# Planning a kernel's order with longer elementwise steps, longer hops, later landings and new priorities

## The chip, the cores and the metric

The kernel runs on one core of one Trainium2 chip. The metric is device microseconds (us) of one execution; the time of a kernel is the median of its runs, and lower is better.

## The reference

Causal attention with a cumulative bias, then two feed-forward layers, all in float32. Batch 4, 8 heads, 576 positions, head width 64, so 2304 tokens of width 512; the feed-forward width is 2048.

```python
scores = scale * np.matmul(q, k.transpose(0, 1, 3, 2))
cum = np.cumsum(np.maximum(s, 0.0), axis=-1)
bias = -(cum[:, :, :, None] - cum[:, :, None, :])
scores = np.where(causal, -1000000000.0, scores + np.minimum(bias, 0.0))
attn = softmax(scores); x = attn @ v           # heads side by side: 2304 x 512
h = x @ w_in;  x = (h * clip(h + 3, 0, 6) / 6) @ w_out       # layer 1
h = x @ w2_in; out = mish(h) @ w2_out                        # layer 2
```

## The kernel before

The tokens are laid out in an order of their own, in five blocks of 512, 512, 384, 512 and 384 tokens. Blocks 0 and 1 hold positions 0 to 255 of the four batches (two batches each), blocks 2 to 4 positions 256 to 575.

**Attention** goes by pairs of heads. `small` (L572) does a pair for positions 0 to 255: scores on TensorE (L610), bias and row minimum on VectorE (L622), exponentials on ScalarE (L629), a reciprocal (L637, L638), the division by it on either engine (L647 ScalarE, L649 VectorE), transposes on TensorE (L655), their copies out of PSUM (L290 or L294), the product with V (L664), and a copy of its result into the block as a high and a low half (L290, L674). GpSimd masks the bias (L596) that a DMA has brought from the scratch tensor `cums`. `unit` (L424) does the same for positions 256 to 575 (scores L486, minimum L493, exponentials L501, transposes L532, V product L555); its result goes out to the scratch tensor `xs` (L568) and comes back into a block (L697).

**Layers.** A weight slice of 128 x 512 comes as 64-bit words and is split into a high and a low part by `load_split` (L328): L339 or L341, L345, L349, L355, then L290 or L294, L365. A slice has 16 numbers f; the first layer's come through `load_win` (L377) and `load_wo1`. `moe_step` (L713) does one slice of one block: the first product, four chunks of three matmuls (L722), the nonlinearity on ScalarE and VectorE (L733, L735 and L740, then L290 or L294, L743), and the second product, again chunks of three (L755 in layer 1, L760 in layer 2). Chunk c of the first product needs rows c of the block, that is head pair c of both batches in it. The chunks of the first product are chained, so nothing of slice 1 starts before the last chunk of slice 0.

**The order.** Nothing is issued in the order of the source. `Plan` collects nodes, each with an engine or a choice of two, a cost in us, a priority (smaller is earlier) and buffers, and `run` (L116 on) simulates them greedily: whenever an engine is free in its simulation it takes the ready node of smallest priority. The order that comes out is the program's order on each engine; on the chip each engine then follows its order and waits on semaphores. The costs and the simulated clock go nowhere else. A node's end is start plus cost; a dependent node is ready after a table value for the pair of engines plus `HOP`; a DMA ends 0.907 us after its share of a simulated ring. In the first 60 simulated us matmuls cost 1.6 times as much. Elementwise costs come from formulas: `v1x(n)` is 0.069 + 0.00104 n, `act(n)` 0.094 + 0.000833 n; the table says 0.128 from VectorE to ScalarE and 0.2 from either to TensorE.

**Priorities** are counted in units of 128 token columns of one slice; a slice of a 512 block is 4 units. They come from the numbers T: head pair k of the first batch has -100 + 2 k `sm`, of the second -100 + 8 `sm` + 2 k `sm2`, weight slice f of w_in -100 + `w0` + `w1` f (its elementwise steps one less, its load four less). After these 8 pairs come six windows of pairs with start `p0` to `p5` and length `s0` to `s5`. In a pair, `upre`/`spre` place the loads and the preparation ahead of its scores, `uhalf`/`shalf` its transposes and `upost`/`spost` its V product behind them, in steps of that window; TensorE's nodes of attention count 5.322 (`pe`) less. First products of block 0 begin at priority -12, those of block 2 at 119.

The first three lines below set the priorities of the first 8 pairs and of the w_in slices (L827, L829), the rest those within a pair (L436, L437, L576).

```python
units(*u, PRO + 8 * k * T["sm"], T["sm2"] if k else T["sm"], n0, ...)
load_win(0, f, PRO + T["w0"] + T["w1"] * f, [n0])
pre = prio - T["upre"] * step
half, post = prio + T["uhalf"] * step, prio + T["upost"] * step
pre, half, post = prio - T["spre"] * step, prio + T["shalf"] * step, prio + T["spost"] * step
```

Of the kernel before, what the change touches and what calls it, by code (L numbers as in the profile page):

```python
# [31 lines left out]
CTOT = sum(CW)  # L32

T = dict(
    sm=3.895, sm2=5.532, w0=5.919, w1=9.308, cum=14.045, wo=0.564, blk0=27.645, blk1=12.97, wo2=44.236,
    wo2r=11.978, win2=5.088, g=30.578, upre=6.511, uhalf=1.145, upost=3.306, uv=0.304, spre=6.035, shalf=0.728,
    spost=1.158, pe=5.322, bias=2.302, la=3, la2=2, wp=11.079, p0=-8.796, p1=2.0, p2=2.856,
    p3=65.354, p4=87.114, p5=119.475, s0=30.881, s1=22.0, s2=23.277, s3=36.84, s4=66.006, s5=29.106,
)
HOP = 0.05  # L40
BIAS = {"DVE": T["bias"]}


# [23 lines left out]
class Plan:  # L67
# [56 lines left out]
    def run(self):  # L124
        for n in self.nodes:
            n.left = len(n.deps)
            n.ready = 0.0
            for d in n.deps:
                d.succ.append(n)
        self.turn = {}  # L130
        news = [(n.prio if b.key is None else b.key, n.seq, b) for n in self.nodes for b in n.new if not isinstance(b, Bank)]
        for _, _, b in sorted(news, key=lambda x: x[:2]):
            self.turn.setdefault(b.tag, collections.deque()).append(b)
        engines = sorted({e for n in self.nodes for e in n.eng})
        free = {e: 0.0 for e in engines}
        pool = []
        for n in self.nodes:
            if n.left == 0:
                pool.append(n)
        done = []  # L140
        now = 0.0
        order = []
        ring = 0.0
        left = len(self.nodes)
        pool.sort(key=lambda n: (n.prio, n.seq))
        while left:
            progress = True
            while progress:
                progress = False
                for n in pool:  # L150
                    if n.ready > now + 1e-9:
                        continue
                    best = None
                    for e, c in zip(n.eng, n.cost):
                        w = c * BIAS.get(e, 1.0)
                        w += 0.989 * max(0.0, free[e] - now)
                        if best is None or w < best[2]:
                            best = (e, c, w)
                    if best is None or free[best[0]] > now + 1e-9 or not self.can(n):
                        continue  # L160
                    self.take(n)
                    e, c, _ = best
                    if e == "PE" and now < 60.0:
                        c *= 1.6
                    free[e] = now + c
                    n.end = now + c
                    if e == "SP":
                        ring = max(now + 1.1, ring) + n.lat
                        n.end = ring + 0.907
                    else:  # L170
                        n.end += n.lat
                    n.on = e
                    order.append((n, e))
                    pool.remove(n)
                    heapq.heappush(done, (n.end, n.seq, 0, n))
                    heapq.heappush(done, (n.end + 0.252, n.seq, 1, n))
                    left -= 1
                    progress = True
                    break
            times = [t for t in free.values() if t > now + 1e-9]  # L180
            times += [n.ready for n in pool if n.ready > now + 1e-9]
            if done:
                times.append(max(done[0][0], now))
            if not times:
                raise RuntimeError("stuck: " + ", ".join(str((n.prio, n.eng, [b.tag for b in n.new])) for n in pool[:8]))
            now = min(times)
            changed = False
            while done and done[0][0] <= now + 1e-9:
                _, _, kind, n = heapq.heappop(done)
                if kind:  # L190
                    self.drop(n)
                    continue
                for m in n.succ:
                    m.left -= 1
                    m.ready = max(m.ready, n.end + (0.0 if n.on == "SP" else HOPS.get((n.on, m.eng[0]), 0.12) + HOP + m.slack))
                    if m.left == 0:
                        pool.append(m)
                        changed = True
            if changed:
                pool.sort(key=lambda n: (n.prio, n.seq))  # L200
        self.total = now
        self.order = order
        for n, e in order:
            for b in n.new:
                if isinstance(b, Bank):
                    b.t = self.bank_pool.tile([P, 512], F32, tag=f"b{b.tag}", name=f"b{b.tag}")
                else:
                    p = b.pool() if callable(b.pool) else b.pool
                    b.t = p.tile(b.shape, b.dtype, tag=b.tag, name=b.name)
            n.fn(e) if len(n.eng) > 1 else n.fn()  # L210
# [718 lines left out]
```

## Time and profile before

| | |
|---|---|
| median of 3 runs | 1002.32 us (1001.36 to 1003.06) |
| the profiled execution | 1003.14 us, span 1001.4 us |
| TensorE busy | 982.1 us of the span, 98% |
| VectorE, ScalarE busy | 462.4 us, 476.9 us (46%, 48%) |
| chain that ended last | TensorE 95%, VectorE 2%, DMA 1%, ScalarE 1% |

The span runs from the first to the last instruction of the profiled execution; the 1.7 us by which its time is longer lie around it. Engine names in rows: PE is TensorE's matmuls, PEld its weight loads, DVE VectorE, ACT ScalarE, POOL GpSimd, SP SyncE. An L number is a line of the kernel. A row says out<-in by the program's tile names; b is a PSUM bank.

### The profile page before, as it was taken

What the parts mean: (1) busy time and instruction counts of PE and PEld (TensorE: products, weight loads), DVE (VectorE), ACT (ScalarE), POOL (GpSimd) and SP (SyncE); (2) the same over time, 40 slices, a digit from 0 to 9 for tenths busy, and PEclk for the clock granted to TensorE, in tenths of its full rate; (3) what the DMA queues carried; (4) which work ended last, traced back from release to release, by engine and by line L of the source; (5) the groups of instructions that cost most, each with busy time, mean ns of one, the idle gap of its engine ahead of it and who ended that gap; (6) DMA issues with size and microseconds to landing.
All of it is one profiled execution on the core that took longest, in us unless ns stands there. A gap on an engine that the chain in (4) does not pass through costs nothing.

```text
span 1001.4 us, 13786 instructions
## 1 busy us (share of the span) xinstructions
PE 982.1 (98%) x5016; PEld 803.8 (80%) x5016; DVE 462.4 (46%) x1067; ACT 476.9 (48%) x1008; POOL 44.1 (4%) x102
## 2 busy tenths in 40 slices
PE   6899999999999999999999999999999999999998
PEld 3567777777777798888889998888888888888996
DVE  7898887754544455435228879612112112111111
ACT  5887778675665555644226556323123223122222
POOL 1111110100010101000000000000000000000000
PEclk9799999999999999999999999999999999999999
DMA  8676876887566777466237785202001101000101
GB/s 274 199 256 239 275 229 228 276 262 216 168 199 195 233 219 216 138 237 220 85 122 251 254 270 187 84 1 74 1 1 43 43 1 63 1 1 1 43 1 32
DMA packets 60355, 146.05 MB, mean 146 GB/s; under 512 B 8352, under 2 KB 22720, under 8 KB 60288
## 3 DMA queue, kind: packets, MB, share of 16 engines
q1 hardware_dynamic: 60288, 145.17, 44.6%
q8 instruction: 40, 0.66, 0.3%
q14 instruction: 27, 0.22, 0.1%
HBM read 121.84 MB, written 23.31 MB: 145 GB/s over the span
## 4 chain that ended last, share of the span: by engine, by line
PE 95%; DVE 2%; DMA 1%; ACT 1%; issue 0%; SPq 0%; DVEq 0%; ACTq 0%
PE b L722 40%; PE b L755 20%; PE b L760 20%; PE b L486 4%; PE b L555 4%; PE b L532 3%; PE b L610 2%; PE b L664 1%; PE b L655 1%; DMA xs<-st 1%; DMA blk<-xs 0%; PE b L613 0%; DVE g L622 0%; DMA pt<-in_s_dram 0%; DVE win L365 0%
## 5 line engine op out<-in xcount | busy, mean ns | idle before, releaser
L722 PE MATMUL b<-blk,win 128*128 128x512 f32 (+1 forms) x1920 | 505.5, 373 | 0.3 <-DMA blk<-xs 0.3
L722 PEld LDWEIGHTS b<-blk,win 128*128 128x128 f32 x1920 | 347.0, 188 | 58.6 <-issue 6.6
L755 PE MATMUL b<-g,wo 128*128 128x512 f32 (+1 forms) x960 | 258.7, 378 | 0.0
L755 PEld LDWEIGHTS b<-g,wo 128*128 128x128 f32 x960 | 170.3, 188 | 28.6 <-issue 8.4
L743 DVE TENSOR_TENSOR g<-e,g 128x512 fp32r<-128x512 f32 (+1 forms) x120 | 77.2, 644 | 214.4 <-ACT g L290 213.5
L740 ACT ACTIVATE e<-b 128x512 f32<-128x512 f32 (+1 forms) x80 | 44.4, 555 | 249.4 <-PE b L722 249.2
L760 PE MATMUL b<-wo,wo 128*128 128x512 f32 x432 | 122.1, 391 | 0.0
L760 PE MATMUL b<-wo,g 128*128 128x512 f32 x432 | 122.0, 391 | 0.0
L290 ACT ACTIVATE g<-e 128x512 fp32r<-128x512 f32 (+1 forms) x105 | 62.3, 593 | 74.0 <-PE b L755 72.4
L760 PEld LDWEIGHTS b<-wo,g 128*128 128x128 f32 x432 | 80.5, 188 | 13.3 <-DVE g L743 0.3
L760 PEld LDWEIGHTS b<-wo,wo 128*128 128x128 f32 x432 | 80.6, 188 | 12.9
L743 DVE TENSOR_TENSOR wo<-e,wo 128x512 fp32r<-128x512 f32 (+1 forms) x40 | 25.5, 639 | 131.8 <-ACT wo L290 131.6
L735 DVE SCALAR_TENSOR_TENSOR e<-e,b 128x512 f32<-128x512 f32 (+1 forms) x80 | 50.4, 630 | 59.9 <-ACT e L733 59.3
L501 ACT ACTIVATE cb<-cb,nm 128x384 f32<-128x384 f32 (+2 forms) x80 | 54.4, 682 | 29.9 <-DVE nm L493 29.2
L733 ACT ACTIVATE e<-b,three 128x512 f32<-128x512 f32 (+1 forms) x80 | 51.3, 641 | 31.6 <-DVE g L743 15.7
L493 DVE CUSTOM_DVE_ANT_0 cb<-b,cb 128x384 f32<-128x384 f32 (+2 forms) x80 | 44.7, 588 | 29.3 <-PE b L486 24.1
L290 ACT ACTIVATE pt<-b 128x384 f32<-128x384 f32 (+2 forms) x95 | 48.0, 505 | 19.8 <-PE b L532 18.8
L532 PE MATMUL b<-ident,cb 128*128 128x128 f32 x304 | 48.8, 272 | 0.0
L532 PEld LDWEIGHTS b<-ident,cb 128*128 128x128 f32 x304 | 39.0, 140 | 9.2 <-ACT cb L521 0.2
L486 PE MATMUL b<-qk 64*128 64x384 f32 (+2 forms) x288 | 46.2, 364 | 0.0
L355 DVE SCALAR_TENSOR_TENSOR wtmp<-wraw,wtmp 128x512 uint32<-128x512 uint32 x64 | 44.2, 691 | 1.0
L349 DVE SCALAR_TENSOR_TENSOR wtmp<-wraw,wtmp 128x512 uint32<-128x512 uint32 x64 | 44.1, 690 | 1.2
(77 smaller groups left out, 729.8 us busy)
## 6 DMA issues: line engine op xcount, KB each, us to landing
wo<-wos SPq DMA_DIRECT2D x64, 512.0 KB, 4.0
wraw<-in_w_in_dram SPq DMA_DIRECT2D x32, 512.0 KB, 4.6
wraw<-in_w_out_dram SPq DMA_DIRECT2D x32, 512.0 KB, 4.5
cb<-cuml SPq DMA_DIRECT2D x16, 896.0 KB, 7.8
wos<-wo SPq DMA_DIRECT2D x16, 512.0 KB, 5.3
qkr<-in_qk_dram SPq DMA_DIRECT2D x16, 480.0 KB, 3.6
v<-in_v_dram SPq DMA_DIRECT2D x16, 320.0 KB, 6.9
cb<-cums SPq DMA_DIRECT2D x12, 384.0 KB, 4.5
```

Source lines behind the costliest of these rows:

```text
L290: nc.scalar.activation(out=out_, in_=in_, func=AF.Copy)
L486: nc.tensor.matmul(out=ps[g].t[:, 0:w], lhsT=t.t[s_, ka, qo:qo + P], rhs=t.t[s_, kb, nk0 + a:nk0 + e], start=k == 0, stop=k == 2)
L493: nc.vector.tensor_tensor_reduce(out=p.t[:, o:o + w], in0=pb.t[:, 0:w], in1=cb.t[:, o:o + w], scale=-0.125, scalar=(3.0e38 if a == 0 else ...
L501: nc.scalar.activation(out=p.t[:, o:o + w], in_=p.t[:, o:o + w], func=AF.Exp, scale=-1.0, bias=nm.t[:, k:k + 1], accum_out=l.t[:, k:k + 1],)
L532: nc.tensor.transpose(out=ps.t[:, P * z:P * (z + 1)], in_=p.t[:, o:o + P], identity=ident)
L722: nc.tensor.matmul(out=hps.t[:, 0:N], lhsT=w.t[:, a, P * c:P * (c + 1)], rhs=x.t[:, c, b, :], start=(c == 0 and k == 0), stop=(c == NCC - ...
L733: a = add("ACT", actp(N, 1), lambda: nc.scalar.activation(out=e0.t[:, 0:N], in_=hps.t[:, 0:N], func=AF.Relu, bias=three, scale=1.0), [prev ...
L735: a = add("DVE", v1x(N), lambda: nc.vector.scalar_tensor_tensor(out=e0.t[:, 0:N], in0=e0.t[:, 0:N], scalar=6.0, in1=hps.t[:, 0:N], op0=ALU ...
L740: a = add("ACT", actp(N) + 0.15, lambda: nc.scalar.activation(out=e0.t[:, 0:N], in_=hps.t[:, 0:N], func=AF.Mish), [prev], t, [e0], [hps])
L743: gl = add("DVE", v1x(N), lambda: nc.vector.tensor_tensor(out=g.t[:, 1, 0:N], in0=src.t[:, 0:N], in1=r(g.t[:, 0, 0:N]), op=ALU.subtract), ...
L755: nc.tensor.matmul(out=y[j].t[:, 0:N], lhsT=wt.t[:, a, P * j:P * (j + 1)], rhs=g.t[:, b, 0:N], start=(f == 0 and k == 0), stop=(f == NF - ...
L760: nc.tensor.matmul(out=y[j].t, lhsT=g.t[:, a, P * j:P * (j + 1)], rhs=wt.t[:, b, :], start=(f == 0 and k == 0), stop=(f == NF - 1 and k == 2),
```

## The change

The table T gets new values for 13 of its entries. The constant `HOP` goes from 0.05 to 0.15. In the simulation, a node on any engine but TensorE takes 1.08 times its cost, and a DMA ends 1.5 us behind its ring share in place of 0.907. No instruction is added, removed or resized in the source; which of two engines takes a step, and every engine's order, may come out otherwise.

```diff
 T = dict(
-    sm=3.895, sm2=5.532, w0=5.919, w1=9.308, cum=14.045, wo=0.564, blk0=27.645, blk1=12.97, wo2=44.236,
-    wo2r=11.978, win2=5.088, g=30.578, upre=6.511, uhalf=1.145, upost=3.306, uv=0.304, spre=6.035, shalf=0.728,
-    spost=1.158, pe=5.322, bias=2.302, la=3, la2=2, wp=11.079, p0=-8.796, p1=2.0, p2=2.856,
-    p3=65.354, p4=87.114, p5=119.475, s0=30.881, s1=22.0, s2=23.277, s3=36.84, s4=66.006, s5=29.106,
+    sm=7.035, sm2=5.532, w0=7.467, w1=9.308, cum=14.045, wo=0.346, blk0=27.645, blk1=12.97, wo2=44.236,
+    wo2r=11.978, win2=5.088, g=30.578, upre=4.13, uhalf=1.145, upost=4.65, uv=0.363, spre=6.035, shalf=0.623,
+    spost=1.158, pe=5.322, bias=2.302, la=3, la2=2, wp=11.079, p0=-13.796, p1=1.367, p2=2.856,
+    p3=65.354, p4=87.114, p5=109.294, s0=30.881, s1=22.0, s2=23.277, s3=37.788, s4=50.354, s5=35.089,
 )
-HOP = 0.05
+HOP = 0.15
@@ -162,11 +162,13 @@
                     e, c, _ = best
                     if e == "PE" and now < 60.0:
                         c *= 1.6
+                    elif e != "PE":
+                        c *= 1.08
                     free[e] = now + c
                     n.end = now + c
                     if e == "SP":
                         ring = max(now + 1.1, ring) + n.lat
-                        n.end = ring + 0.907
+                        n.end = ring + 1.5
```

## Rows read from the trace of the kernel before

**Rows 1.** Stretches of 25 us: from:to, length, busy us (instructions) per engine, clock, DMA.

```profile
core 0: us, PE busy (x) PEld busy (x) DVE busy (x) ACT busy (x) POOL busy (x), PEclk, DMA share, GB/s
0.00:25.00 25.00, 15.14 (x51) 9.20 (x52) 17.90 (x58) 13.18 (x38) 4.97 (x16) 0.95 0.85 274
25.00:50.00 25.00, 20.98 (x112) 12.98 (x111) 20.22 (x80) 20.29 (x68) 2.63 (x6) 0.70 0.61 199
50.00:75.00 25.00, 24.67 (x119) 15.48 (x119) 23.22 (x70) 21.73 (x64) 3.02 (x6) 1.00 0.78 255
75.00:100.00 25.00, 25.00 (x131) 18.49 (x128) 21.16 (x56) 18.25 (x44) 3.51 (x6) 1.00 0.70 241
...
975.00:1000.00 25.00, 21.57 (x105) 18.56 (x104) 2.79 (x5) 6.88 (x13) 0.00 (x0) 0.98 0.11 32
```

**Rows 2.** PE's waits, whole span: who waited for whom, us in total, times, longest.

```profile
PE b L655 <- ACT g L647: 3.6, 2, 3.1
PE b L610 <- DMA qkr<-in_qk_dram: 3.6, 1, 3.6
PE b L655 <- ACT cb L647: 2.0, 1, 2.0
...
PE b L613 <- DVE pt L323: 0.9, 1, 0.9
...
PE b L722 <- DMA blk<-xs: 0.3, 1, 0.3
```

**Rows 3.** The chain that ended last: start us, us, engine and line, instructions.

```profile
28.59 1.58 PE b L610 x4
...
71.34 0.85 PE b L610 x4
72.19 0.89 PE b L722 x3
...
840.22 2.06 PE b L722 x9
```

**Rows 4.** Engines in time: start us, us, engine, line, operation [idle before, releaser].

```profile
10.34 0.69 DVE L355 SCALAR_TENSOR_TENSOR wtmp<-wraw,wtmp 128x512 uint32<-128x512 uint32 x1
...
11.07 0.63 ACT L290 ACTIVATE win<-wtmp 128x512 fp32r<-128x512 f32 x1
```

**Rows 5.** TensorE in time, 36 to 47 us.

```profile
36.58 1.51 PE L655 MATMUL b<-ident,cb 128*128 128x128 f32 x6 [0.94 <-DVE cb L649]
...
45.57 0.52 PE L655 MATMUL b<-ident,cb 128*128 128x128 f32 x3 [1.42 <-issue]
45.85 0.94 PE L722 MATMUL b<-blk,win 128*128 128x512 f32 x3
```

**Rows 6.** Stretches of 2 us, columns as in the first group.

```profile
22.00:24.00 2.00, 0.21 (x1) 0.18 (x1) 1.97 (x13) 1.89 (x8) 0.77 (x2) 0.68 1.01 358
24.00:26.00 2.00, 1.68 (x7) 1.09 (x7) 1.76 (x6) 2.00 (x8) 0.00 (x0) 0.50 0.30 115
...
28.00:30.00 2.00, 2.00 (x7) 1.11 (x5) 1.23 (x3) 0.67 (x2) 0.11 (x1) 0.50 0.71 262
...
38.00:40.00 2.00, 2.00 (x13) 1.25 (x14) 0.57 (x4) 1.18 (x3) 0.00 (x0) 0.56 0.28 103
```

**Rows 7.** Weight-split steps, whole span, by shape: busy us, mean ns | idle before, releaser.

```profile
L355 DVE SCALAR_TENSOR_TENSOR wtmp<-wraw,wtmp 128x512 uint32<-128x512 uint32 x64 | 44.2, 691 | 1.0
...
L345 DVE TENSOR_SCALAR wtmp<-wtmp 128x512 uint32<-128x512 uint32 x64 | 27.4, 428 | 10.2 <-ACT wtmp L339 9.6
...
L365 DVE TENSOR_TENSOR win<-wtmp,win 128x512 fp32r<-128x512 f32 x32 | 22.2, 694 | 3.9 <-ACT win L290 3.6
```

**Rows 8.** The chain that ended last, where block 2 begins: start us, us, what.

```profile
320.17 0.02 issue
...
322.68 5.22 DMA xs<-st
...
327.96 4.83 DMA blk<-xs
```

## The prediction

> **What bounds the kernel now.** I read the stretches of 25 us first. From 75 us to 975 us there are 36 stretches, and TensorE is busy in all of every one but one, around block 2's start, at the granted clock of 1.00, which is the 2.4 GHz level; VectorE and ScalarE have room from there on [rows 1]. So no order of the elementwise steps can gain there unless TensorE itself has less to do. The list of its waits says the same: beyond 75 us it names a single wait, 0.3 us [rows 2]. A busy TensorE is not a TensorE at its peak, so the chain comes next. A run of nine matmuls of the first product takes 2.06 us, 0.69 for three, while three that stand between attention's matmuls take 0.89 [rows 3]. An alternation therefore costs some 0.2 us, and the change could move it only by changing how often attention and layers alternate.
>
> What is left is the start. In 0 to 25, 25 to 50 and 50 to 75 us TensorE is idle for 9.86, 4.02 and 0.33 us, 14.2 in all [rows 1]. Of the first stretch, three waits lie ahead of any choice of order: 3.6 us for the first load of q and k, 0.9 for the prefix sums, 3.1 for the softmax of the very first pair [rows 2]. That makes 7.6 and leaves 6.6 us of idle that an order can reach. The end has its own idle, 3.4 us in the last full stretch [rows 1], for which no edit is aimed and whose two layers' worth of priorities (la2, g, wo2, win2) are unchanged.
>
> **The change, part by part.** Nothing is emitted anew: costs, HOP and the landing time of a DMA exist in the simulation alone. They have no price of their own; they act through the order, the choice between ScalarE and VectorE included.
>
> *Costs and hops.* Is the plan of before too fast? One link shows that it is not. L355 takes v1x(512) = 0.069 + 0.00104 x 512 = 0.60 us in the plan, and a ScalarE step behind it is ready 0.128 + 0.05 later: 0.78 us from start to start. The trace has 10.34 to 11.07, 0.73 us [rows 4]. With 1.08 and the longer hop it becomes 0.65 + 0.28 = 0.93. So the change is no correction, it is slack, about 0.2 us for each hop: a dependent step is put behind other work that is ready. Slack pays where TensorE waits for a step that came a little late with something else to do in its stead. That is the stretch from 25 to 50 us, in which the longest gaps are 0.94 us for a division on VectorE and 1.42 us between pairs [rows 5]. The 2.0 us wait at 22 to 24 us [rows 2] stays, since VectorE has 1.97 and ScalarE 1.89 of those 2 us filled [rows 6]. In 25 to 50 us VectorE has 4.78 and ScalarE 4.71 us free [rows 1], so there is elementwise time in which the late steps could be done. Bounds: a gain of 6.6 us, all the reachable idle, at one end; at the other a loss, worked out as the first rival. I take three quarters of the 4.02 us idle of 25 to 50 us, 3.0 us, because the gaps shown there are short and stand beside free elementwise time; the last quarter I leave for the first chunk of each pair, which has nothing to go in front of it.
>
> *sm and w0: weights against attention.* By the formulas, the second batch's first pair moves from -100 + 8 x 3.895 = -68.8 to -43.7, its last from -35.6 to -10.5. Weight slice f stands at -95.1 + 9.31 f before and -93.5 + 9.31 f after (its elementwise steps). So three slices go ahead of that first pair before and six after; seven go ahead of the last pair before and nine after. One split costs VectorE 0.428 + 0.691 for L355 and as much for L349 + 0.694 = 2.50 us [rows 7], three of them 7.5 us. The 4.78 us that VectorE has free in 25 to 50 us take 4.8 of these; 2.7 us must show somewhere. If the first pairs of window 0 (TensorE work of the same kind) stand in for what comes later, it hides; if that cover is gone, it costs its 2.7 us. I cost it at nothing in the forecast and carry the rest into the first rival. Each slice moved brings its load on SP's queue with it, ahead of the q and k loads of later pairs; the two raw buffers (wraw) hold no more than two loads at a time, which bounds that.
>
> *p0, p1.* Window 0's first pair goes from -8.8 to -13.8, which is ahead of the last pair of block 0 (-10.5 now, -35.6 before). Its TensorE work fills the start, its VectorE work stands before the pair that block 0 still needs: no net price in the forecast.
>
> *upre, upost, s3, s4, p5, s5.* Loads and preparation of the later pairs come 2.4 steps closer to their scores, their V products 1.3 steps later. All of that lies where TensorE has other work in every microsecond [rows 1]. One place has no margin: block 2 begins right behind the store of the last V product it needs (5.22 us) and its load (4.83 us), and TensorE waits 0.3 us for it [rows 2, 8]. For that pair the V product's priority is 3.306 x 36.84 / 8 = 15.2 behind its scores before, 4.65 x 37.788 / 8 = 22.0 after. Bounds: the 0.3 us gone at one end; at the other 6.7 units, at 1.38 us for one (a slice of 512 has eight chunks of 0.69 us in four units [rows 3]), 9.2 us. I take 0: the V product ends at 320.17 us, 2.5 us ahead of its store [rows 8], and what could come in its way by the new priority is chunks of 0.69 us. wo, uv and shalf shift things by under half a unit or a tenth of a step: nothing.
>
> *Alternations.* A pair of `unit` has 11 TensorE nodes; 16 of them and the 8 later pairs of `small` at 5 make 216. At up to 0.2 us each, a shift of a tenth in how many are parted would be 4 us, either way. No edit joins or parts them, so I take 0 and keep 1 us in the range.
>
> *The clock.* From within 22 to 24 us to within 38 to 40 us the granted clock is 0.50, the 1.2 GHz level [rows 6]; four score matmuls of a pair take 1.58 us there and 0.85 later [rows 3]. It fell in a stretch with 0.21 us of TensorE work in 2. TensorE is then busy for 2.00 of every 2 us from 26 to 34 us (four stretches like the one shown), and still has 0.50. The eight stretches from 24 to 40 us hold 14.7 us of TensorE work, which at the other level would be 14.7 x 0.85 / 1.58 = 7.9, so 6.8 us less. Bounds: a gain of 6.8 us if the clock does not fall, a loss of a few us if it falls a second time at the gap ahead of 45.57 us [rows 5]. The Trainium skill ("TensorE: Matmul & The Clock Gate", Part 1) says that the throttled state is the default and that sustained activity releases it. By that rule a denser start would have its clock back soon after 26 us, and the sum would be up to 6.8 us lower; the trace does not agree, since a full 8 us of busy time brought nothing back. I take no change in the sum.
>
> **The sum.** 1003.14 - 3.0 (gaps) - 0 (weights, windows, block 2, alternations, clock) = 1000.1 us against the profiled execution, which is 0.82 us above the median. Against the median that is 999.3 us, and this is the forecast. Its own range is 995.7 (all 6.6 us) to 1000.3.
>
> **The rivals.**
>
> *First, slower: the start becomes bound by VectorE.* Place: from 25 to 65 us. Three more splits ahead of the second batch's pairs (2.7 us beyond VectorE's free time) and window 0's first pair ahead of the last one (its VectorE work, about the same 2.5 us) put the first complete slice of block 0 later by up to 5.2 us. For it: VectorE is at 23.22 of 25 in 50 to 75 us [rows 1], and first products are what closes TensorE's gaps from 45.85 us on [rows 5]. Against it: nearly 5 us free in 25 to 50. It decides from the point at which the first L722 stands after 45.85 + 2.7 = 48.6 us. Time: 1002.3 + 5.2 = 1007.5 at most; 1005 as its middle. Chance 0.24.
>
> *Second, no difference.* The edits change an order and TensorE is full from 75 us on; greedy filling may give the start the same gaps at other places. Up to 2 us either way, 1002.3 us. It is also the case in which the change does not do what it says. Chance 0.22.
>
> *Third, faster by the clock.* If the gap at 22 to 24 us shrinks, the clock may not fall. Half to all of 6.8 us beside the gaps: 992.5 to 995.9 us. Against it: the elementwise engines are full just there. Chance 0.12.
>
> *Fourth, slower at block 2.* The V product of the last pair comes late by part of the 9.2 us: 1004 to 1008 us. For it: no margin today. Against it: a node of smaller priority must stand ready at that moment to pass it. Chance 0.06.
>
> The forecast keeps 0.36. A difference of 0.2%, 2 us, is about what a measurement of this kernel tells from none. Faster: 0.36 + 0.12 = 0.48; same 0.22; slower 0.24 + 0.06 = 0.30. Cases of both signs hold the chance, so the range goes from 993 (the clock's case without its best end) to 1007.5 (the first rival's end, the fourth's without its worst).
>
> **What would show it.** Right: TensorE's idle in 25 to 50 us near 1 us, with the first L722 no later than 46 us and the wait list of 75 us on still empty. First rival: that first L722 behind 48.6 us, VectorE near 25 of 25 in 25 to 75 us, and more TensorE idle there. Clock: the granted clock of 25 to 50 us over 0.70. Block 2: a wait of over 1 us for blk<-xs around 330 us. Wrong altogether: a difference that lies beyond 75 us with neither a wait nor block 2 in it, which would point to the alternations.

## The result, and the profile after

The changed kernel takes 1010.28 us (median of 4 runs, 1008.88 to 1011.54) beside 1002.69 us for the one before: a ratio of 1.0076, 95% interval 1.0063 to 1.0088. It is 7.6 us slower, outside the range of the prediction. (In the changed kernel and in those made from it, lines behind the edit stand two numbers higher: L612 is L610 of before, L724 is L722.)

The stretches of 25 us of the changed kernel, columns as in [rows 1]:

```profile
0.00:25.00 25.00, 14.46 (x52) 8.46 (x52) 16.51 (x56) 12.88 (x39) 4.98 (x16) 1.00 0.76 254
25.00:50.00 25.00, 22.32 (x91) 13.22 (x92) 20.20 (x73) 20.11 (x65) 2.95 (x6) 0.58 0.65 216
50.00:75.00 25.00, 22.38 (x98) 14.14 (x97) 16.72 (x55) 17.16 (x51) 2.73 (x6) 0.74 0.64 196
75.00:100.00 25.00, 24.57 (x126) 17.21 (x127) 20.37 (x57) 20.35 (x53) 5.57 (x6) 1.00 0.80 269
100.00:125.00 25.00, 25.00 (x141) 18.60 (x139) 20.97 (x52) 18.28 (x43) 1.21 (x2) 1.00 0.49 169
```

From 100 us on every stretch up to 1000 us is full, so the loss lies in front of that. TensorE's idle time there is 10.54 + 2.68 + 2.62 + 0.43 = 16.3 us, against 14.2 [rows 1]. That is 2.1 us of some 8. The rest is longer busy time, and the clock column shows one reason for it: 0.58 and 0.74 where before had 0.70 and 1.00 [rows 1]. In stretches of 2 us it falls three times, not once [rows 6]:

```profile
32.00:34.00 2.00, 2.00 (x12) 0.81 (x10) 1.13 (x9) 1.98 (x9) 0.00 (x0) 0.50 0.76 277
...
40.00:42.00 2.00, 1.28 (x7) 0.86 (x7) 1.92 (x8) 2.00 (x7) 0.77 (x2) 1.00 1.02 383
...
50.00:52.00 2.00, 2.00 (x7) 1.07 (x6) 1.52 (x8) 1.42 (x5) 0.00 (x0) 0.50 0.00 0
...
58.00:60.00 2.00, 2.00 (x9) 1.22 (x10) 2.00 (x11) 2.00 (x8) 0.00 (x0) 1.00 0.78 180
...
64.00:66.00 2.00, 1.56 (x9) 0.74 (x5) 1.03 (x3) 0.88 (x3) 0.00 (x0) 0.50 0.80 285
```

The half level holds from about 25.6 to 39.3, 42.7 to 56.3 and 63.2 to 70 us, 34 us in all, against 17. Ahead of the first fall the column can't be trusted: it shows 1.00, but in the kernel before six transposes take as long at 15.11 us as at 23.79 us, where it shows 0.50:

```profile
15.11 1.73 PE L655 MATMUL b<-ident,g 128*128 128x128 f32 x6 [3.07 <-ACT g L647]
...
23.79 1.73 PE L655 MATMUL b<-ident,cb 128*128 128x128 f32 x6 [2.02 <-ACT cb L647]
```

So the first pair ran at half speed as well. The changed kernel has 1.78 us there (at 14.73 us), so this start is alike in both. What the half level does to the work, TensorE in time, 46 to 68 us:

```profile
46.33 2.12 PE L724 MATMUL b<-blk,win 128*128 128x512 f32 x3 [0.49 <-ACT blk L292]
...
51.43 1.65 PE L612 MATMUL b<-qkr 64*128 64x128 f32 x4
...
58.73 0.92 PE L612 MATMUL b<-qkr 64*128 64x128 f32 x4
...
63.18 1.55 PE L666 MATMUL b<-qk 128*64 128x256 f32 x8 [1.98 <-ACT qk L292]
...
66.70 1.63 PE L724 MATMUL b<-blk,win 128*128 128x512 f32 x3
```

Four score matmuls take 1.65 us at the half level and 0.92 at the full one. The line at 66.70 (this view ends at 68 us) starts with the fourth chunk of the first product, with which the first slice of block 0 is complete, so that the next slice can begin. Before, that chunk is here:

```profile
58.25 0.97 PE L722 MATMUL b<-blk,win 128*128 128x512 f32 x3
```

The delay of 8.4 us is as large as the growth of the span (1001.4 to 1009.8): from this chunk to the end both take 943.1 us. The chunk waits for the last of block 0's eight pairs, whose last copy into the block is here, before and after:

```profile
57.87 0.41 DVE L674 TENSOR_TENSOR blk<-b,blk 128x256 fp32r<-128x256 f32 x1
```

```profile
65.20 0.42 DVE L676 TENSOR_TENSOR blk<-b,blk 128x256 fp32r<-128x256 f32 x1 [0.97 <-ACT blk L292]
```

The fifth of these eight copies starts at 45.48 us before and at 46.76 us after, so most of the delay arises behind it. The weights, which were to profit, are no earlier: the last step of a w_in split, counted up to 60 us, before and after:

```profile
L365 DVE TENSOR_TENSOR win<-wtmp,win 128x512 fp32r<-128x512 f32 x10 | 7.0, 704 | 0.2
```

```profile
L367 DVE TENSOR_TENSOR win<-wtmp,win 128x512 fp32r<-128x512 f32 x9 | 6.2, 686 | 0.0
```

### The profile page after: what moved, and what is told of

Read it like the earlier page. It is cut to its first block, busy times and chain, and to the rows that moved or that the text cites. A ratio compares the mean times of both kernels' runs of the same rounds, so it can differ in the third digit from the quotient of the medians.

```text
span 1009.8 us, 13812 instructions
## 1 busy us (share of the span) xinstructions
PE 988.4 (98%) x5016; PEld 807.2 (80%) x5016; DVE 461.4 (46%) x1071; ACT 473.8 (47%) x1004; POOL 48.4 (5%) x102
## 4 chain that ended last, share of the span: by engine, by line
PE 96%; ACT 1%; DMA 1%; DVE 1%; issue 0%; SPq 0%; POOL 0%; ACTq 0%; POOLq 0%
PE b L724 40%; PE b L757 20%; PE b L762 20%; PE b L488 4%; PE b L557 3%; PE b L534 3%; PE b L612 3%; PE b L657 1%; PE b L666 1%; DMA wraw<-in_w_out_dram 0%; PE b L615 0%; ACT cb L631 0%; DMA cb<-cums 0%; DMA pt<-in_s_dram 0%; ACT qk L292 0%
## 5 line engine op out<-in xcount | busy, mean ns | idle before, releaser
L724 PE MATMUL b<-blk,win 128*128 128x512 f32 (+1 forms) x1920 | 505.9, 375 | 0.6 <-ACT blk L292 0.5
L724 PEld LDWEIGHTS b<-blk,win 128*128 128x128 f32 x1920 | 348.3, 188 | 60.2 <-issue 7.6
```

The source lines that it names most:

```text
L724: nc.tensor.matmul(out=hps.t[:, 0:N], lhsT=w.t[:, a, P * c:P * (c + 1)], rhs=x.t[:, c, b, :], start=(c == 0 and k == 0), stop=(c == NCC - ...
```

## The experiments

Ratios are to the kernel before on the same chip, with 95% intervals.

**Which part.** The simulation's edits with the old table (e1, the diff of the change without T), the new table with the old simulation (e2, T alone), the changed kernel with the start's priorities put back (e3), and these alone in the kernel of before (e4):

```diff
# e3, on the changed kernel (three entries of T, the others of their lines left out);
# e4 is the reverse, on the kernel of before
-    sm=7.035,  w0=7.467,  p0=-13.796
+    sm=3.895,  w0=5.919,  p0=-8.796
```

> The three edits of the simulation alone (1.08, HOP 0.15, landing 1.5) with the table T of before. If the start priorities (sm, w0, p0) cause the loss, this stays near before: 1000 to 1004 us, half clock for some 17 us of the first 75. If the slack of the simulation causes it, by placing each dependent step later than the chip needs, this takes 1008 to 1011 us with over 25 us of half clock.

Measured: 1005.53 us, 1.0034 (1.0021 to 1.0047).

> The new table T alone, with the simulation of before (no 1.08, HOP 0.05, landing 0.907). Start priorities as the cause: 1007 to 1011 us, as the changed kernel. Slack as the cause: 1001 to 1004 us. If only both together do it, this and the run with the simulation alone are both near 1003.

Measured: 1009.65 us, 1.0070 (1.0049 to 1.0091).

> The changed kernel with sm, w0 and p0 put back to 3.895, 5.919 and -8.796; all else as changed. Start priorities as the cause: back to 1001 to 1004 us, with first products from 46 us on closing the gaps and half clock near 17 us. Slack as the cause: stays at 1008 to 1011 us.

Measured: 1010.9 us, 1.0076 (1.0060 to 1.0091).

> The kernel of before with sm, w0 and p0 alone set to 7.035, 7.467 and -13.796. Start priorities as the cause: 1006 to 1011 us, clock falling two or three times before 75 us. Slack as the cause: 1001 to 1004 us.

Measured: 1009.0 us, 1.0052 (1.0037 to 1.0067).

So the table without the slack costs as much as the whole change, within the intervals; the slack without the table costs 0.34%, which lies in neither range that was expected for it; and the start's priorities by themselves cost 5 us. e3 is the odd one: start put back, loss still whole. Its trace shows a new loss for most of it; stretches of 5 us, TensorE in time, and its wait:

```profile
335.00:340.00 5.00, 3.99 (x18) 2.98 (x16) 0.00 (x0) 2.39 (x4) 0.00 (x0) 1.00 0.80 239
340.00:345.00 5.00, 2.98 (x9) 2.98 (x10) 0.55 (x1) 0.99 (x2) 0.00 (x0) 0.62 0.98 326
345.00:350.00 5.00, 5.00 (x22) 5.00 (x22) 2.43 (x5) 1.02 (x3) 0.00 (x0) 0.70 0.68 258
```

```profile
342.02 6.66 PE L724 MATMUL b<-blk,win 128*128 128x384 f32 x21 [3.04 <-DMA blk<-xs]
```

This is block 2 of [rows 8], which in this order comes 3 us late, and the clock falls on top of it: 21 matmuls of 384 columns take 6.66 us, where nine of them late in the span of before take 1.56, which would be 3.6:

```profile
831.84 1.56 PE b L722 x9
```

By this estimate a gap of 3 us costs about 6. Putting upost back too (e5) tests that the V products' later place made it:

```diff
# e5, on e3
-    upost=4.65
+    upost=3.306
```

> The changed kernel with sm, w0, p0 and upost put back. With sm, w0 and p0 alone put back it took 1010.9 us, and its trace had a 3.0 us wait for block 2 with 6.8 us of half clock behind it, about 5 us. If upost (V products 1.3 steps later) makes that wait, it is gone here: 1004.5 to 1007 us, as the simulation's edits alone. If not upost: 1009 to 1012 us.

Measured: 1006.66 us, 1.0052 (1.0032 to 1.0073). The wait is gone, and 4.2 us with it; its stretch is

```profile
325.00:350.00 25.00, 25.00 (x149) 19.73 (x149) 15.58 (x41) 16.35 (x36) 1.41 (x4) 1.00 0.74 229
```

**sm, and a control.** sm alone, in both kernels (g1 sets it in that of before, e6 puts it back in the changed one), then in one of its two places (s1), and a control that moves HOP by a hundredth:

```diff
# s1, on the kernel of before
-            units(*u, PRO + 8 * k * T["sm"], ...
+            units(*u, PRO + 8 * k * 7.035, ...
# d1, on the kernel of before
-HOP = 0.05
+HOP = 0.06
```

> The kernel of before with sm alone at 7.035: the second batch's pairs of block 0 stand 25 units later, behind three more weight slices. If this is what delays the first complete slice of block 0 (12 matmuls of it done at 58.8 us before, 65.7 with sm, w0 and p0 together), it does so here too and costs 3 to 6 us: 1006 to 1009. If p0 (window 0's pairs ahead of the last pair) is what does it: 1002 to 1004.

Measured: 1008.3 us, 1.0059 (1.0042 to 1.0075).

> The changed kernel with sm alone put back to 3.895. If sm carries the loss of the start (sm alone in the kernel of before cost 5.6 us): 1004 to 1007 us, and the first complete slice of block 0 near 60 us in place of 67.7. If w0 and p0 do as much without it: 1008 to 1011 us.

Measured: 1005.65 us, 1.0032 (1.0018 to 1.0047), its ten runs from 1003.17 to 1009.53.

> The kernel of before with sm = 7.035 in one of its two places only: the start of the second batch's pairs (-43.7 in place of -68.8), the spacing of the first batch's pairs left at 3.895. If the lateness of the second batch is what sm costs: 1006.5 to 1009 us, first slice of block 0 after 61 us. If the wider spacing of the first batch is: 1002 to 1004 us.

Measured: 1011.91 us, 1.0093 (1.0078 to 1.0108).

> The kernel of before with HOP 0.06 in place of 0.05, a hundredth of a microsecond, as a control: it reorders about half of TensorE's program, with no aim at all. If the named edits (sm, p0, the size of the slack) cause the loss, this stays at 1002 to 1004 us. If the time of before is a lucky order that any other greedy order falls behind, 1005 to 1009 us.

Measured: 1006.39 us, 1.0034 (1.0021 to 1.0048), its ten runs from 1002.52 to 1007.96.

sm is worth 4.6 us in the changed kernel and 5.6 in that of before. The later start of the second batch's pairs alone is enough to cost that; it costs 9.7 us (s1), more than was expected and more than sm in both places, so the two places do not add up. Its profile has the clock at 0.52 in 25 to 50 us. The other edits leave 3.2 us (e6), and the one reordering with no aim costs as much (d1). That loss goes with the clock: d1's two runs at a mean granted clock of 0.994 take 1002.5 and 1003.0 us, its six at 0.987 to 0.989 take 1006.2 to 1008.0. Whether other aimless orders lose as much was not tried.

**The clock.** Order or clock? Each of the next kernels has the order of its parent on every engine and some spare matmuls more on TensorE, whose result nobody reads. The first two ran them ahead of waiting transposes (one group of f2 ahead of a V product), in the bank of these (f1, f2); the next two behind the matmuls before the gap, in unused columns of their bank (f3, f4); the last ones there too, but in a bank of their own (f5 and f7 in the changed kernel, f6 in that of before, f8 in e6). FILL gives their number at each place; the rest of the edits is left out:

```diff
# f1, f2: at five and seven places
+        for _ in range(FILL.get((kind, seen[kind]), 0)):
+            nc.tensor.matmul(out=bank.t[:, 0:512], lhsT=w[:, 0, 0:P], rhs=w[:, 0, 0:512], start=True, stop=True)
...
# f5 to f8: behind the score, transpose or V product node ahead of the gap (f3, f4: out=bank.t[:, 384:512])
+            for _ in range(k):
+                nc.tensor.transpose(out=spare[0][:, 0:P], in_=ident, identity=ident)
...
-        all8 = [6, 7, 4, 5, 0, 1, 2, 3]
+        all8 = [6, 7, 4, 5, 0, 1, 2]
```

> The kernel of before, its order untouched, with 21 extra matmuls of 512 columns on the first weight slice, whose result is overwritten, ahead of five transposes of the first pairs where TensorE waited (3, 8, 3, 2 and 5 of them). They add no data the kernel needs. If the half clock between 23 and 40 us follows from the gaps, it vanishes or shrinks: of the 14.7 us that TensorE worked there some 5 to 7 come off, less what the fillers take beyond the gaps (0 to 3): 997 to 1001 us. If the clock does not follow the gaps, 1003 to 1008 us.

Measured: 1000.73 us, 0.9980 (0.9971 to 0.9989), with the clock column at 1.00 all through the profiled run.

> The changed kernel, its order untouched, with 33 such fillers at its own gaps (ahead of the transposes at 14.7, 23.6, 35.0, 40.7, 60.4 and 66.2 us and the V product at 63.2 us). If the half clock (34 us of it in the profiled run) is the price of the change, most of the 8 us come back: 1000 to 1004 us. If the idle time and the order themselves are the price and the clock is a bystander: 1010 to 1016 us.

Measured: 1012.91 us, 1.0112 (1.0093 to 1.0131). It tells nothing: the first large group waited for its bank and then ran at the half level, in the way of the transposes:

```profile
24.02 5.49 PE L411 MATMUL b<-win 128*128 128x512 f32 x12 [3.03 <-DVE nm L633]
```

> The kernel of before, its order untouched, with 49 spare transposes of the identity into unused columns of a bank, each group right behind the matmuls after which TensorE had waited (12, 16, 6, 3, 8 and 4 of them), so that they wait for nothing and fill the gap. As a cure of the clock without the delay of the first fillers, which stood ahead of the waiting transposes: 997 to 1000 us and no half clock between 23 and 50 us. If transposes do not hold the clock: 1003 to 1006 us with the half clock still there.

Measured: 1002.68 us, 1.0006 (0.9997 to 1.0015). The clock column is at 1.00 here too, but no time came of it, which neither expectation had foreseen: the first pair's transposes start at 17.68 us, 2.6 us later than before.

> The changed kernel, its order untouched, with 66 such spare transposes behind the matmuls after which it waited (10, 22, 5, 8, 3, 14 and 4). The first try at this waited for a free bank and stood in the way for over 5 us; these do not. If the half clock is most of the price: 1001 to 1005 us with under 10 us of half clock. If the lateness of the pairs themselves is the price: 1008 to 1011 us even with the clock at full.

Measured: 1010.38 us, 1.0087 (1.0072 to 1.0102). The clock was up for most of the start (0.996 in the mean of the profiled run, 0.86 in 25 to 50 us), but the steps that read a bank waited for the spare work in it. The first pair's transposes, at 14.73 us in the changed kernel, came at 17.26:

```profile
11.91 2.40 PE L412 MATMUL b<-ident 128*128 128x128 f32 x10
17.26 1.78 PE L669 MATMUL b<-ident,g 128*128 128x128 f32 x6 [2.95 <-ACT g L661]
```

> The kernel of before, every engine's order untouched, with 49 spare transposes into a bank of their own behind the matmuls after which TensorE had waited. If its half clock (some 17 us in most runs) costs 0.35 to 0.4 us for each us, as the spread of its own runs says: 996.5 to 999.5 us. If the chain of the pairs would set the time even at the full clock: 1000 to 1002 us.

Measured: 999.39 us, 0.9972 (0.9962 to 0.9983), below both kernels.

> The changed kernel, every engine's order untouched, with 65 spare transposes behind the same matmuls as in the second try, but into a bank that nobody else has in this stretch, so that no step of VectorE or ScalarE waits for them. Clock theory (the half clock is most of the price): full clock and 1001 to 1005 us. Chain theory (the pairs come late because of the order, and a faster TensorE then waits for ScalarE and VectorE): 1006 to 1010 us although the clock is at full, with more idle plus spare time on TensorE in the first 75 us.

Measured: 1005.38 us, 1.0032 (1.0021 to 1.0044), with 13.7 us of half clock left.

> As the third try on the changed kernel, with 87 spare transposes in place of 65 (18 for 5, 9 for 7 and 8 for 3 behind the third to fifth V product), since that run still had 13.7 us of half clock around 34 and 48 us. If the half clock left there carried what stood between it (1005.4) and the kernel of before held at full clock (999.4): 1000 to 1002.5 us. If the order carries it: 1003.5 to 1006 us with the clock at full.

Measured: 1003.65 us, 1.0011 (1.0000 to 1.0022).

> The changed kernel with sm put back and 63 spare transposes at its own gaps. Its runs without them spread from 1003.2 us (mean granted clock 0.992) to 1009.5 (0.985). If that spread and its distance from before are the clock alone: 997 to 1000.5 us, as the kernel of before held at full clock (999.4). If w0, p0 and the rest make an order that is worse in itself: 1002 to 1005 us.

Measured: 1002.34 us, 1.0004 (0.9992 to 1.0015).

The stretches of the kernel of before with spare matmuls (f6), and of the changed one (f7), the spare work among TensorE's busy time:

```profile
0.00:25.00 25.00, 19.36 (x78) 12.63 (x78) 17.82 (x58) 13.22 (x38) 5.14 (x16) 1.00 0.86 273
25.00:50.00 25.00, 22.66 (x153) 14.88 (x153) 24.19 (x91) 24.02 (x82) 4.88 (x8) 1.00 0.75 246
50.00:75.00 25.00, 24.75 (x121) 16.44 (x121) 23.17 (x68) 21.03 (x58) 2.06 (x6) 1.00 0.83 256
```

```profile
0.00:25.00 25.00, 19.69 (x86) 13.09 (x86) 16.52 (x57) 12.94 (x40) 4.72 (x16) 1.00 0.76 254
25.00:50.00 25.00, 22.48 (x156) 15.52 (x156) 23.59 (x86) 23.54 (x75) 3.60 (x6) 1.00 0.73 239
50.00:75.00 25.00, 23.23 (x129) 16.09 (x129) 20.52 (x66) 20.94 (x63) 3.25 (x7) 1.00 0.73 249
```

In both the clock column is at 1.00; the first pair's transposes still take 1.73 and 1.78 us, so what the spare work kept is the clock behind 20 us. The first slice of block 0 is complete here, in f6 and in f7:

```profile
54.07 0.96 PE L740 MATMUL b<-blk,win 128*128 128x512 f32 x3
```

```profile
59.26 1.63 PE L742 MATMUL b<-blk,win 128*128 128x512 f32 x6
```

And this is the spare work in them, by group:

```profile
L415 PE MATMUL b<-ident 128*128 128x128 f32 x49 | 7.9, 313 | 0.0
```

```profile
L417 PE MATMUL b<-ident 128*128 128x128 f32 x87 | 12.0, 293 | 0.0
```

Idle and spare time together are 8.2 + 7.9 = 16.1 us in f6 and 9.6 + 12.0 = 21.6 in f7. Those 5.5 us are about what TensorE waits longer at the full clock in the changed order; what of them is spare work standing in the way was not measured.

The division of the loss follows, as an estimate. With the clock held on both sides the changed kernel stands at 1.0011 / 0.9972 = 1.0039 of the one before, 3.9 us. Left to themselves they differ by 7.6. So about 3.9 us are the order's and 3.7 the clock's, each within some 1.6 us by the intervals and if the 87 spare matmuls of f7 and the 49 of f6 cost alike: holding it gives the changed kernel 6.5 us and the one before 2.8. sm belongs mostly to the second part: it costs 4.6 us with the clock left alone (changed kernel against e6), and with the clock held 1.3 (f7 against f8), which their intervals do not tell from none.

## Why the prediction was wrong

**What bounds the kernel** stood: from the first slice's last chunk on, both kernels take 943.1 us.

**The gaps, 3.0 us of gain**, is the term of the sum that failed first: slack was to bring other ready work into the gaps, and the runs show a later order instead. Idle of 25 to 50 us did shrink, from 4.02 to 2.68 us, but not by more work in it: the stretch ran 91 matmuls where before it ran 112, and more of them at the half level. Idle grew by 0.68 us in 0 to 25, by 2.29 in 50 to 75 and by 0.43 in 75 to 100, so that in all it is 2.1 us more. The slack alone (e1) was 0.34% slower, and with the clock held the changed order is 3.9 us slower where 3.0 of gain was put.

**The clock, taken at 0,** is the second term that failed, with about 3.7 us of loss. The text saw the way to it ("a loss of a few us if it falls a second time at the gap ahead of 45.57 us") and counted it nowhere, neither among the rivals nor in the range. It fell a second and a third time. I had also turned down the rule of the Trainium skill ("TensorE: Matmul & The Clock Gate", Part 1) that activity releases the throttle, because 8 busy us at 0.50 [rows 6] spoke against it. With the gaps filled the clock did not fall again (f6, f7), which shows what keeps it up and not what brings it back. What in those 8 us kept it down is open; attention's small matmuls were all that ran. The bound of 6.8 us for a clock that does not fall was too large as well: f6 gained 2.8 us.

**sm and w0, costed at nothing:** sm measured 5.6 us alone in the kernel of before; w0 was not tried alone. The first rival had the place and the sign, and a delay of the first slice (5.2 us at most, measured 8.4), but its mechanism was wrong in the main. VectorE did not fill up: 16.72 us of 50 to 75, where before had 23.22 [rows 1]. Ahead of the last pair's copy (57.87 and 65.20 us) the traces have 9 splits ended before and 10 after, one more and not two. And its point of decision, a first L722 behind 48.6 us, was not met: it stands at 46.33, and what came late is the fourth chunk, at 66.70. The first slice waits for the last pair, and meanwhile TensorE has little but pairs, for much of the time at half its clock. The bound of the range, 1007.5, left out that a late pair is also a slower one. Which steps of the last pair the new order puts back, apart from the clock, was not followed up.

**p0, alternations, the tail.** p0 was not tried alone. The equal 943.1 us behind the first slice leave no net loss for alternations or the tail.

**Block 2, taken at 0 with a rival of 0.06:** right for the change itself, where no wait for it is left. But the mechanism is there: e3 showed it at 3.0 us, and e5 that upost makes it. Why the changed kernel, which has upost too, has no such wait was not tested; its other edits shift the same stretch.

**No difference and "greedy filling" (0.22)**: the control d1 speaks against the way this case was thought of. The one reordering with no aim that was run did not come out at the old time: by its ratio it costs 3.4 us, and its runs spread over 5.4 us with the clock.

## To carry to other kernels

Before costing a new order, look for the stretch in which one engine has no spare work: there a lateness goes to the end one to one, and on TensorE it is paid a second time in clock. One aimless perturbation cost 3.4 us here, so run a few of them before a loss of that size is put down to an edit. Where TensorE must wait for a chain of small steps, spare matmuls in a bank of their own, behind the last matmul before the gap, were worth 2.8 us here; in unused columns of a bank that others read they gave nothing (f3).

## What the runs showed of the hardware

Runs of one and the same program differ, and in e6 and d1 the slower ones were granted less clock. Ten runs of e6 go from 1003.17 us at a mean granted clock of 0.992 to 1009.53 at 0.985: by this estimate 2 x 0.007 x 1005 = 14 us more at the half level go with 6.4 us of time. The kernel of before stays within 1000.33 and 1004.66 in all of its runs.

The clock fell in the middle of the kernel too, behind a gap of 3.0 us at 339 us (e3), although TensorE had been full from 200 to 335 us. The Trainium skill describes such a fall in its page "TensorE: Matmul & The Clock Gate", section "HAM oscillation — how this bites in real kernels": a wait for data throttles the clock, and the work behind the wait starts slowly.
